# A spectral mix and a gated dense layer: early dense products spread over three phases, gates' loads and a gating product moved

## The chip, the cores and the metric

The kernel runs on one core of one Trainium2 chip. The metric is the device time of one execution in microseconds (us); lower is better. The engines are TensorE (PE), which multiplies; VectorE (DVE) and ScalarE (ACT), which split, add and evict; GpSimd (POOL) and SyncE (SP), which here only issue transfers, each through a queue of its own.

## The reference, cut to what matters

```python
x = A_x                                        # 1 x 2048 x 640
g = sigmoid((x * gate_w).sum(-1, keepdims=True))
a = einsum("bsd,ed->bse", x, dft_hid_re)
b = einsum("bsd,ed->bse", x, dft_hid_im)
y = einsum("ts,bse->bte", dft_seq_re, a) - einsum("ts,bse->bte", dft_seq_im, b)
h = einsum("bsd,df->bsf", x, w1) + b1          # 640 -> 1728
act = h * tanh(softplus(h))                    # mish
return g * y + (1 - g) * einsum("bsf,fd->bsd", act, w2)
```

All arrays are fp32.

## The kernel before, in words

**Stages.** The work is transposed: features lie on the 128 partitions, tokens in four groups t of 512 columns. Four stages follow each other on PE. The sequence stage multiplies x with the cosine and sine matrices (`sq`, four problems q: two halves of the tokens, real and imaginary part) and stores `usc`. The hidden stage (`hd`, two problems, one for each half of the tokens) multiplies that with the hidden matrices and stores y (`ysc`). The dense stage (`dense_first`, L816) makes the activations `asc`. The last stage (`ou`, two problems) multiplies them with w2, adds y and writes the output. Each problem is a two by two block product with seven instead of eight products (Winograd's form), so many operands are sums and differences that DVE makes. Each fp32 operand is split into a high and a low part in fp32r (`operand` L326, `split` L316: a copy on ACT, then a difference on DVE), and each product is three matmuls (`mm3` L341: high by high, high by low, low by high).

**A problem's phases.** `first` (L414) makes the product b11 and the fifth block row, over kh steps of k, into three banks, and copies them out (`to_sbuf` L313); with `aside` they go to HBM and come back later. `second` (L438) has three products (22, s2, s1), and prepares the lower weights for each k in `low` (L381): two loads into tiles of the pool x, four differences on DVE, five splits. `third` (L508) has the last three; its `done` (L555) and `give` (L563) evict the results, with a product by q where `q` is given: in the hidden stage that is g of the token group, broadcast over the partitions.

**The early part.** A share of the dense stage, that of the first six feature blocks (of 128) of w1 for the token groups 0 and 1, is computed between the first phases of the sequence stage. The order on PE is: sq[1].first, early_first (L730), sq[2].first, early_second (L762), sq[3].first, early_rests (L812), sq[0].first, and then second and third of each q. early_first has three units j of seven products over two of the five k; its results go to HBM (`early`). early_second has three units over the other three k, loads `early` back, adds, applies mish (`out_act` L662) and stores. `turns` (L725) lets the three units take one step each in turn. A unit of early_first uses three banks (b0, b1, b2), one of early_second four; PSUM has eight. `w1_twice` (L688) loads blocks of w1, forms sums t1 to t4 in tiles of the pool f, and splits them; `x_twice` (L712) does the same for x.

**Gates.** `gates` (L909) loads the gate weights once (`wide`) and x in token order in sixteen tiles of the pool x; one DVE instruction (L915) multiplies each by `wide` and sums it. g and 1 - g go to HBM as rows, from which they are broadcast.

**What sets the order.** All is written into a graph (`Graph` L48), and a planner (`run` L124) plays it forward with costs: a matmul 0.2267 us, ACT and DVE by their columns, a transfer 2.2 us plus its size at 370 GB/s. PE's order is that of the program. On ACT, DVE and the queues of SP and POOL the planner issues, whenever an engine is free, the ready operation with the earliest due time (`want`, worked out backwards from PE's times) for which tiles are free. The chip then executes each engine's instructions in that order. `by` sets a latest time by hand; gates' products have `GATES[0] + k * GATES[1]` = 120 + 10 k. Tiles are taken from pools in the plan: eight banks `psum`, 18 `f` (512 columns), 6 `x` (640 columns), 26 weight pairs `w`, 10 operand pairs `r`.

Of the kernel before, what the change touches and what calls it, by code (L numbers as in the profile page):

```python
# [12 lines left out]
OP = mybir.AluOpType  # L13
# [14 lines left out]
DELAY, RATE = 2.2, 370e3  # L28
GATES = 120.0, 10.0

# [8 lines left out]
class Op:  # L39


    def __init__(self, engine, emit, took, hold, at):
        self.engine, self.emit, self.took, self.hold, self.at = engine, emit, took, hold, at
        self.deps, self.after, self.vals = set(), [], []
        self.prompt, self.ends, self.want, self.psum, self.by = False, 0.0, None, False, 1e9


class Graph:  # L48
# [35 lines left out]
    def wants(self):  # L84
# [35 lines left out]
        for op in self.ops:  # L120
            if op.engine != "PE":
                op.want = max([op.want] + [(d.at if d.engine == "PE" else d.want) + d.took for d in op.deps])

    def run(self, pools):  # L124
# [22 lines left out]
        events, now, left, dma = [], 0.0, len(self.ops), 0.0  # L147

        def granted(op, blocked):
# [17 lines left out]
        while left:  # L167
            began = False
            for e, line in ready.items():
                if free[e] > now + 1e-9 or not line:  # L170
                    continue
                if e == "PE":
                    i = next((i for i, x in enumerate(line) if x[1] == pe[-1]), None)
                    if i is not None and not granted(self.ops[pe[-1]], set()):
                        i = None
                else:
                    blocked = set()
                    i = next((i for i, x in enumerate(line) if granted(self.ops[x[1]], blocked)), None)
                if i is None:
# [16 lines left out]
                else:  # L196
                    end = now + op.took + 0.03
                heapq.heappush(events, (end, op.n))
                left -= 1
                began = True  # L200
            if began:
                continue
            times = [t for e, t in free.items() if t > now + 1e-9 and ready[e]]
            if events:
                times.append(events[0][0])
            assert times, ("stuck", left, pe and self.ops[pe[-1]].at, [(p.name, len(p.free)) for p in pools])
            now = max(now, min(times))
            while events and events[0][0] <= now + 1e-9:
                op = self.ops[heapq.heappop(events)[1]]
# [18 lines left out]
def fnet_mish_gate(ctx: ExitStack, tc: tile.TileContext, xn, xt, c_re, c_im, wd_re, wd_im,  # L228
# [51 lines left out]

    def load(pool, src, of=None, rows=P, cols=N, queue="SP", by=1e9):
        v = Val(pool)
        op = dma(queue, lambda: ISSUE[queue].dma_start(v.t[:rows, :cols], src() if callable(src) else src),  # L283
                 whole(of) if of else [], whole(v), rows * cols * 4)
        op.by = by
        return v
# [119 lines left out]
    class Problem:  # L406
# [281 lines left out]
    def w1_twice(k0, fifth=False):  # L688

        C, w, at, n, tiles = slice(0, H * P), {}, {}, 0, []  # L690
        for i in range(2):
            for j in range(2):
                w[f"b{i + 1}{j + 1}"] = load(FS, w1h[k0 + i, j], cols=H * P)
        for o, x, y in (("t1", "b12", "b11"), ("t2", "b22", "t1"), ("t3", "b22", "b12"), ("t4", "b21", "t2")):
            w[o] = Val(FS)
            tt(w[o], w[x], w[y], OP.subtract, (C, C, C), n=H * P)
        if fifth:
            for j in range(2):
                w["d", j] = load(FS, w1h[KD - 1, j], cols=H * P)
        for o in ("b11", "b21", "t2", "t1", "t3", "t4", "b22") + (("d", 0), ("d", 1)) * fifth:  # L700
            i = 0
            while i < H:
                if n % KD == 0:
# [20 lines left out]

    def turns(units):  # L725
        units = list(units)
        while units:
            units = [u for u in units if next(u, u) is None]

    def early_first():  # L730

        at, x = w1_twice(0), x_twice(0)

        def unit(j):
            b0, b1, b2 = bank(), bank(), bank()
            mm3(b0, at["b11", j], x["a11"], True, True)
            p = to_sbuf(b0)
            yield
            mm3(b2, at["t1", j], x["s1"], True, True)
            yield  # L740
            mm3(b0, at["b21", j], x["a12"], False, True)
            store(early[0, j], to_sbuf(b0))
            yield
            copy(b1, p)
            mm3(b1, at["t2", j], x["s2"], False, True)
            u = to_sbuf(b1)
            yield
            mm3(b1, at["t3", j], x["s3"], False, True)
            v = to_sbuf(b1)
            tt(v, b2, v, OP.add)  # L750
            store(early[1, j + H], v)
            yield
            mm3(b1, at["t4", j], x["a22"], False, True)
            store(early[1, j], to_sbuf(b1))
            yield
            mm3(b2, at["b22", j], x["s4"], False, True)
            tt(u, b2, u, OP.add)
            store(early[0, j + H], u)
            yield
        turns(unit(j) for j in range(H))  # L760

    def early_second():  # L762
# [4 lines left out]
        def unit(j):  # L767
            b0, b1, b2, b3 = bank(), bank(), bank(), bank()

            def end(b, t, f):  # L770
                o = load_of(FS, early[t, f])
                tt(o, b, o, OP.add)
                out_act(f, t, o, o)
            mm3(b0, at["b11", j], x["a11"], True, True)
            p = to_sbuf(b0)
            yield
            mm3(b0, at["b21", j], x["a12"], False, False)
            mm3(b0, at[("d", 0), j], d[0], False, True)
            end(b0, 0, j)
            yield  # L780
            copy(b1, p)
            mm3(b1, at["t2", j], x["s2"], False, True)
            u = to_sbuf(b1)
            o = load_of(FS, early[0, j + H])
            tt(u, u, o, OP.add)
            yield
            mm3(b2, at["t1", j], x["s1"], True, True)
            yield
            mm3(b1, at["t3", j], x["s3"], False, True)
            v = to_sbuf(b1)  # L790
            tt(v, b2, v, OP.add)
            yield
            mm3(b1, at["t4", j], x["a22"], False, False)
            mm3(b1, at[("d", 0), j], d[1], False, True)
            end(b1, 1, j)
            yield
            mm3(b2, at["b22", j], x["s4"], False, False)
            mm3(b2, at[("d", 1), j], d[0], False, True)
            tt(u, b2, u, OP.add)
            out_act(j + H, 0, u, u)  # L800
            yield
            copy(b3, load_of(FS, early[1, j + H]))
            mm3(b3, at[("d", 1), j], d[1], False, True)
            tt(v, b3, v, OP.add)
            out_act(j + H, 1, v, v)
            yield
        turns(unit(j) for j in range(H))
        kept.update(x, d=d)

    kept = {}  # L810
# [98 lines left out]
    def gates():  # L909

        wide = load(X, gw.partition_broadcast(P), cols=D)
        tokens = xn.rearrange("k p d -> (k p) d").rearrange("(p k) d -> k p d", k=KS)
        for k in range(KS):
            x = load(X, tokens[k], cols=D)
            dve(lambda k=k, x=x: nc.vector.scalar_tensor_tensor(  # L915
# [23 lines left out]
    def put_out(d, t, f, queue=None):  # L939
# [5 lines left out]
    hd = [Problem(hid, tp, lambda t, k: load_of(FS, usc[k][t]), put_y, aside=aside("ph") if tp else None,  # L945
                  q=lambda t: keep(("g", t), lambda: broadcast(grow, t))) for tp in range(2)]
    ou = [Problem(fin, tp, lambda t, k: load_of(FS, asc[k][t]), put_out, rest=out_rest, aside=aside("po") if tp else None,
                  y=(lambda d, t: load_of(FS, ysc[d][t])) if tp else None,
                  q=None if tp else (lambda t: keep(("q", t), lambda: broadcast(qrow, t))), last=tp == 1) for tp in range(2)]
# [17 lines left out]
    for p in hd:  # L967
        p.second(hid.low)
        p.third()
    w1_rest(True)  # L970
    dense_first(0)
# [53 lines left out]
```

## Time and profile before

| | |
|---|---|
| median of three runs | 872.07 us (869.6 to 874.72) |
| the profiled execution | 874.41 us, of which the span from its first to its last instruction is 872.3 us |
| granted clock, mean | 0.996 |
| HBM traffic | 171.97 MB read, 42.22 MB written |

Times in rows of the profile are counted from the span's start. A row of the timeline has the start, the duration, the engine, the line, and the output and inputs by their tiles' names (f, x, w, r as the pools; ps is a bank; h and l are the high and the low part), and in brackets how long the engine had stood and what ended that. L337 is the matmul inside `mm`; L310 the ACT copy inside `copy`; L301 the DVE instruction inside `tt`; L331 and L332 the two halves of `operand`; L322 and L323 those of `split`; L283 a load, L293 a store.

### The profile page before, as it was taken

How to read it: one execution, taken by the hardware profiler on the slowest of the kernel's cores; microseconds unless marked ns; L12 is line 12 of the kernel's file. 1: busy time of each engine (PE TensorE's matmuls, PEld its weight loads, DVE VectorE, ACT ScalarE, POOL GpSimd, SP SyncE). 2: the span in 40 equal slices, each digit the busy share in tenths (PEclk: the TensorE clock that was granted, in tenths of full speed). 3: DMA queues.
4: the chain of work that ended last, by engine and by line, in shares of the span. 5: the costliest groups of instructions: out<-in, count | busy, mean ns of one | idle time of the engine just before them, and what ended most of it. 6: DMA issues, size and time to landing. Idle time of an engine off the chain costs nothing.

```text
span 872.3 us, 12120 instructions
## 1 busy us (share of the span) xinstructions
PE 859.0 (98%) x3754; PEld 705.2 (81%) x3754; DVE 697.2 (80%) x1241; ACT 485.9 (56%) x896; POOL 86.5 (10%) x157
## 2 busy tenths in 40 slices
PE   8998999999999999999999999999999999999998
PEld 6876888888888888888887888878888788888886
DVE  7888799987884887679998868998877996758493
ACT  7976486635353554456676634646666854533242
POOL 0312100002000200100020002022111200004000
PEclk9998999999999999999999999999999999999999
DMA  9999985867763966495677839587666886637943
GB/s 329 323 322 357 368 314 163 291 220 264 251 223 114 340 200 217 132 363 189 221 254 274 314 128 351 196 290 261 230 205 239 279 279 223 193 127 167 355 172 121
DMA packets 108704, 215.01 MB, mean 246 GB/s; under 512 B 13600, under 2 KB 17824, under 8 KB 108640
## 3 DMA queue, kind: packets, MB, share of 16 engines
q1 hardware_dynamic: 95744, 174.52, 59.0%
q0 software_dynamic: 12752, 39.59, 13.3%
q8 instruction: 29, 0.48, 0.2%
q14 instruction: 35, 0.29, 0.1%
q10 hardware_dynamic: 144, 0.13, 0.0%
HBM read 171.97 MB, written 42.22 MB: 246 GB/s over the span
## 4 chain that ended last, share of the span: by engine, by line
PE 87%; DVE 6%; DMA 4%; issue 1%; ACT 1%; SPq 0%; POOL 0%; ACTq 0%; DVEq 0%
PE ps L337 87%; DVE f L301 2%; DMA f<-in_c_im_dram 1%; DMA x<-in_w_dram 1%; DMA f<-in_xt_dram 1%; DMA ps<-f 1%; DVE x L301 1%; DMA f<-early 0%; ACT f L310 0%; DVE r1l L332 0%; DVE w13l L323 0%; SPq L283 0%; DVE w16l L323 0%; DVE r5l L332 0%; DVE w19l L323 0%
## 5 line engine op out<-in xcount | busy, mean ns | idle before, releaser
L301 DVE TENSOR_TENSOR f<-f,f 128x512 f32<-128x512 f32 (+2 forms) x327 | 218.1, 681 | 12.1 <-ACT f L606 4.2
L310 ACT ACTIVATE f<-ps 128x512 f32<-128x512 f32 x138 | 79.4, 595 | 24.6 <-PE ps L337 20.1
L301 DVE TENSOR_TENSOR f<-ps,f 128x512 f32<-128x512 f32 x108 | 70.8, 683 | 23.7 <-PE ps L337 17.0
L293 POOL DMA_DIRECT2D u<-f x40 | 21.6, 542 | 320.0 <-DVE f L301 309.3
L331 ACT ACTIVATE r1h<-f 128x512 fp32r<-128x512 f32 x40 | 25.2, 630 | 27.5 <-PE ps L337 16.5
L293 POOL DMA_DIRECT2D act<-f x52 | 28.2, 543 | 121.9 <-ACT f L606 53.4
L331 ACT ACTIVATE r3h<-f 128x512 fp32r<-128x512 f32 x38 | 23.9, 629 | 28.5 <-PE ps L337 18.4
L331 ACT ACTIVATE r2h<-f 128x512 fp32r<-128x512 f32 x39 | 24.5, 628 | 27.1 <-PE ps L337 18.9
L331 ACT ACTIVATE r8h<-f 128x512 fp32r<-128x512 f32 x38 | 23.9, 630 | 27.9 <-PE ps L337 16.2
L331 ACT ACTIVATE r6h<-f 128x512 fp32r<-128x512 f32 x37 | 23.3, 629 | 26.2 <-PE ps L337 19.1
L331 ACT ACTIVATE r0h<-f 128x512 fp32r<-128x512 f32 x39 | 24.5, 628 | 23.1 <-PE ps L337 11.5
L332 DVE TENSOR_TENSOR r0l<-f,r0h 128x512 fp32r<-128x512 f32 x40 | 27.5, 687 | 12.3 <-ACT r0h L331 12.1
L331 ACT ACTIVATE r5h<-f 128x512 fp32r<-128x512 f32 x38 | 23.9, 629 | 22.6 <-PE ps L337 13.0
L331 ACT ACTIVATE r7h<-f 128x512 fp32r<-128x512 f32 x39 | 24.5, 628 | 19.9 <-PE ps L337 9.7
L301 DVE TENSOR_TENSOR x<-x,x 128x256 f32<-128x256 f32 (+1 forms) x80 | 33.5, 434 | 2.4 <-DMA x<-in_w_dram 1.7
L331 ACT ACTIVATE r9h<-f 128x512 fp32r<-128x512 f32 x37 | 23.3, 629 | 21.2 <-PE ps L337 16.9
L332 DVE TENSOR_TENSOR r3l<-f,r3h 128x512 fp32r<-128x512 f32 x38 | 26.1, 687 | 11.0 <-ACT r3h L331 10.8
L332 DVE TENSOR_TENSOR r7l<-f,r7h 128x512 fp32r<-128x512 f32 x39 | 26.8, 687 | 9.9 <-ACT r7h L331 9.4
L310 ACT ACTIVATE ps<-f 128x512 f32<-128x512 f32 x57 | 33.5, 595 | 1.9 <-DVE f L301 1.7
L332 DVE TENSOR_TENSOR r2l<-f,r2h 128x512 fp32r<-128x512 f32 x39 | 26.8, 687 | 9.6 <-ACT r2h L331 9.2
L606 ACT ACTIVATE f<-f,b1s 128x512 f32<-128x512 f32 x36 | 25.8, 720 | 15.3 <-DVE f L301 14.7
L332 DVE TENSOR_TENSOR r1l<-f,r1h 128x512 fp32r<-128x512 f32 x40 | 27.5, 688 | 8.2 <-ACT r1h L331 7.8
(2225 smaller groups left out, 2689.3 us busy)
## 6 DMA issues: line engine op xcount, KB each, us to landing
f<-in_c_im_dram SPq DMA_DIRECT2D x128, 256.0 KB, 4.1
f<-in_c_re_dram SPq DMA_DIRECT2D x128, 256.0 KB, 4.4
f<-act SPq DMA_DIRECT2D x86, 256.0 KB, 4.3
f<-u SPq DMA_DIRECT2D x80, 256.0 KB, 5.3
act<-f POOLq DMA_DIRECT2D x52, 256.0 KB, 4.6
f<-in_xt_dram SPq DMA_DIRECT2D x42, 256.0 KB, 4.8
u<-f POOLq DMA_DIRECT2D x40, 256.0 KB, 5.2
x<-in_xn_dram SPq DMA_DIRECT2D x24, 320.0 KB, 5.3
```

The lines of the kernel that those rows point to most:

```text
L293: dma(queue, lambda: ISSUE[queue].dma_start(d.t, v.t[:rows]), whole(v), whole(d), rows * N * 4)
L301: dve(lambda: nc.vector.tensor_tensor(o.t[rows, x], a.t[rows, y], b.t[rows, z], op=op), whole(a, b), whole(o), n)
L310: act(lambda: nc.scalar.activation(o.t, a.t, AF.Copy, scale=scale), whole(a), whole(o))
L331: act(lambda: nc.scalar.activation(r.t[0][:, :N], src.t[:, :N], AF.Copy), whole(src), [(r, 0)])
L332: dve(lambda: nc.vector.tensor_tensor(r.t[1][:, :N], src.t[:, :N], f32(r.t[0][:, :N]), op=OP.subtract), whole(src) + [(r, 0)], [(r, 1)])
L337: G.add("PE", lambda: nc.tensor.matmul(bank.t, w.t[wn][:, k * P:k * P + P], x.t[xn_][:, :N], start, stop, skip_group_check=True), [(w, (k, ...
L606: act(lambda: nc.scalar.activation(o.t[rows], src.t[rows], AF.Mish, **more), whole(src, table) + whole(b1s) * bias, whole(o), more=0.1)
```

## The change

- **The early products.** early_first and early_second no longer run as blocks of their own. They return their units, and `first` becomes a generator (`steps`) that yields after each k. Two lines of units, [a0, a2, b1] and [a1, b0, b2] (a of early_first, b of early_second), take one step each after each k of the first phases of sq[2], sq[3] and sq[0]. early_rests comes after all of them.
- **Banks.** A unit has two banks, a and b. Where b1 was opened with a copy of p, now a itself is evicted and p copied back into it. The product t4 comes last, and the last block of early_second accumulates on a copy of v, with `early` added after it instead of before.
- **w1_twice** loads into tiles of the pool x, not f, writes t3 over b12 and t4 over b21, and interleaves sums with splits.
- **Gates.** Their loads have a time `since`, 110 + 10 k, before which the planner doesn't issue them; their products are due at 130 + 10 k.
- **y.** The hidden stage's second problem has no q: its y is stored ungated. `gate_y`, in the program ahead of the dense stage, loads these ten tiles again, multiplies them by g and stores them as `gysc`; due times 600 + 7 i. ou[1] reads `gysc`.
- **The planner** holds an operation of ACT or DVE that becomes ready well ahead of its due time: up to 1 us after an engine's work (CALM), up to 3 us after a transfer (CALM_DMA), less where it is due within 3 us more (NEAR). This changes the order of instructions; it adds none.

```diff
-GATES = 120.0, 10.0
+CALM, CALM_DMA, NEAR = 1.0, 3.0, 3.0
+GATES = 130.0, 10.0
+GATED = 600.0, 7.0
...
-                op.want = max([op.want] + [(d.at if d.engine == "PE" else d.want) + d.took for d in op.deps])
+                op.want = max([op.want, op.since] + [(d.at if d.engine == "PE" else d.want) + d.took for d in op.deps])
...
-                    i = next((i for i, x in enumerate(line) if granted(self.ops[x[1]], blocked)), None)
+                    i = next((i for i, x in enumerate(line)
+                              if self.ops[x[1]].since <= now and granted(self.ops[x[1]], blocked)), None)
...
-                        insort(ready[a.engine], (a.want, a.n))
+                        wait = min(CALM_DMA if op.engine in ("SP", "POOL") else CALM, a.want - now - NEAR)
+                        if a.engine in ("ACT", "DVE") and wait > 0:
+                            heapq.heappush(events, (now + wait, a.n, True))
+                        else:
+                            insort(ready[a.engine], (a.want, a.n))
...
         def first(self, top):
+            for _ in self.steps(top):
+                pass
+
+        def steps(self, top):
...
                     product(banks, blocks, x, k == 0, k == kh - 1)
+                yield
...
-                w[f"b{i + 1}{j + 1}"] = load(FS, w1h[k0 + i, j], cols=H * P)
-        for o, x, y in (("t1", "b12", "b11"), ("t2", "b22", "t1"), ("t3", "b22", "b12"), ("t4", "b21", "t2")):
-            w[o] = Val(FS)
-            tt(w[o], w[x], w[y], OP.subtract, (C, C, C), n=H * P)
+                w[f"b{i + 1}{j + 1}"] = load(X, w1h[k0 + i, j], cols=H * P)
...
+            if o in sums:
+                a, b = sums[o]
+                w[o] = {"t3": w["b12"], "t4": w["b21"]}.get(o) or Val(X)
+                tt(w[o], w[a], w[b], OP.subtract, (C, C, C), n=H * P)
...
     def early_first():
...
         def unit(j):
...
+            a, b = bank(), bank()
+            mm3(a, at["b11", j], x["a11"], True, True)
+            p = to_sbuf(a)
+            yield
+            mm3(b, at["t1", j], x["s1"], True, True)
+            yield
+            mm3(a, at["b21", j], x["a12"], False, True)
+            store(early[0, j], to_sbuf(a))
+            copy(a, p)
+            yield
+            mm3(a, at["t2", j], x["s2"], False, True)
+            u = to_sbuf(a)
+            yield
+            mm3(a, at["t3", j], x["s3"], False, True)
+            v = to_sbuf(a)
+            tt(v, b, v, OP.add)
             store(early[1, j + H], v)
             yield
...
+            mm3(b, at["b22", j], x["s4"], False, True)
+            tt(u, b, u, OP.add)
             store(early[0, j + H], u)
             yield
-        turns(unit(j) for j in range(H))
+            mm3(a, at["t4", j], x["a22"], False, True)
+            store(early[1, j], to_sbuf(a))
+            yield
+        return [unit(j) for j in range(H)]
...
     def early_second():
...
+            mm3(b, at["b22", j], x["s4"], False, False)
+            mm3(b, at[("d", 1), j], d[0], False, True)
+            tt(u, b, u, OP.add)
+            end(u, 0, j + H)
+            yield
+            mm3(a, at["t4", j], x["a22"], False, False)
+            mm3(a, at[("d", 0), j], d[1], False, True)
+            end(a, 1, j)
+            yield
+            copy(b, v)
+            mm3(b, at[("d", 1), j], d[1], False, True)
+            end(b, 1, j + H)
+            yield
...
-        wide = load(X, gw.partition_broadcast(P), cols=D)
+        wide = load(X, gw.partition_broadcast(P), cols=D, since=GATES[0] - 20)
...
-            x = load(X, tokens[k], cols=D)
+            x = load(X, tokens[k], cols=D, since=GATES[0] - 20 + k * GATES[1])
...
-                  q=lambda t: keep(("g", t), lambda: broadcast(grow, t))) for tp in range(2)]
+                  q=None if tp else lambda t: keep(("g", t), lambda: broadcast(grow, t))) for tp in range(2)]
+    gysc = {(d, t): dram(f"gy{d}_{t}") for t in (2, 3) for d in range(KD)}
+
+    def gate_y():
+
+        for i, ((d, t), o) in enumerate(gysc.items()):
+            v = load_of(FS, ysc[d][t])
+            tt(v, v, keep(("g", t), lambda: broadcast(grow, t)), OP.mult)
+            G.ops[-1].by = GATED[0] + GATED[1] * i
+            store(o, v)
...
-    early_first()
-    sq[2].first(seq_top)
-    early_second()
-    sq[3].first(seq_top)
+    ua, ub = early_first(), early_second()
+    lines = [ua[0], ua[2], ub[1]], [ua[1], ub[0], ub[2]]
+    lines = [(u for q in line for u in q) for line in lines]
+    for q in (2, 3, 0):
+        for _ in sq[q].steps(seq_top):
+            for line in lines:
+                next(line, None)
+    for line in lines:
+        for _ in line:
+            pass
     early_rests()
-    sq[0].first(seq_top)
...
+    gate_y()
     w1_rest(True)
```

More of the change, by code (lines that the diff above doesn't have):

```diff
@@ L44, in __init__ @@
         self.deps, self.after, self.vals = set(), [], []
[L45 removed]
+        self.prompt, self.ends, self.want, self.psum, self.by, self.since = False, 0.0, None, False, 1e9, 0.0
 class Graph:
@@ L147, in run @@
         events, now, left, dma = [], 0.0, len(self.ops), 0.0
+        waits = sorted({op.since for op in self.ops})
         def granted(op, blocked):
@@ L197, in run @@
                     end = now + op.took + 0.03
-                heapq.heappush(events, (end, op.n))
+                heapq.heappush(events, (end, op.n, False))
                 left -= 1
@@ L203, in run @@
             times = [t for e, t in free.items() if t > now + 1e-9 and ready[e]]
+            times += [t for t in waits if t > now][:1]
             if events:
@@ L208, in run @@
             while events and events[0][0] <= now + 1e-9:
-                op = self.ops[heapq.heappop(events)[1]]
+                _, n, held = heapq.heappop(events)
+                op = self.ops[n]
+                if held:
+                    insort(ready[op.engine], (op.want, op.n))
+                    continue
                 for v in op.vals:
@@ L279, in fnet_mish_gate, with load @@
     ISSUE = {"SP": nc.sync, "POOL": nc.gpsimd}
-    def load(pool, src, of=None, rows=P, cols=N, queue="SP", by=1e9):
+    def load(pool, src, of=None, rows=P, cols=N, queue="SP", by=1e9, since=0.0):
         v = Val(pool)
@@ L284, in load @@
                  whole(of) if of else [], whole(v), rows * cols * 4)
-        op.by = by
+        op.by, op.since = by, since
         return v
@@ L699, in w1_twice @@
                 w["d", j] = load(FS, w1h[KD - 1, j], cols=H * P)
-        for o in ("b11", "b21", "t2", "t1", "t3", "t4", "b22") + (("d", 0), ("d", 1)) * fifth:
+        sums = {"t1": ("b12", "b11"), "t2": ("b22", "t1"), "t3": ("b22", "b12"), "t4": ("b21", "t2")}
+        for o in ("b11", "b21", "t1", "t2", "t3", "t4", "b22") + (("d", 0), ("d", 1)) * fifth:
             i = 0
+            if o in sums:
+                a, b = sums[o]
+                w[o] = {"t3": w["b12"], "t4": w["b21"]}.get(o) or Val(X)
+                tt(w[o], w[a], w[b], OP.subtract, (C, C, C), n=H * P)
             while i < H:
@@ L723, in x_twice @@
         return x
[L725 to L728, printed above, removed]
     def early_first():
@@ L767, in unit, with end @@
         def unit(j):
-            b0, b1, b2, b3 = bank(), bank(), bank(), bank()
-            def end(b, t, f):
+            a, b = bank(), bank()
+            def end(c, t, f):
                 o = load_of(FS, early[t, f])
-                tt(o, b, o, OP.add)
+                tt(o, c, o, OP.add)
                 out_act(f, t, o, o)
-            mm3(b0, at["b11", j], x["a11"], True, True)
-            p = to_sbuf(b0)
+            mm3(a, at["b11", j], x["a11"], True, True)
+            p = to_sbuf(a)
@@ L776, in unit @@
             yield
-            mm3(b0, at["b21", j], x["a12"], False, False)
-            mm3(b0, at[("d", 0), j], d[0], False, True)
-            end(b0, 0, j)
+            mm3(b, at["t1", j], x["s1"], True, True)
             yield
[L781 to L785, printed above, removed]
+            mm3(a, at["b21", j], x["a12"], False, False)
+            mm3(a, at[("d", 0), j], d[0], False, True)
@@ L786, in unit @@
+            end(a, 0, j)
+            copy(a, p)
             yield
-            mm3(b2, at["t1", j], x["s1"], True, True)
+            mm3(a, at["t2", j], x["s2"], False, True)
+            u = to_sbuf(a)
             yield
-            mm3(b1, at["t3", j], x["s3"], False, True)
-            v = to_sbuf(b1)
-            tt(v, b2, v, OP.add)
+            mm3(a, at["t3", j], x["s3"], False, True)
+            v = to_sbuf(a)
+            tt(v, b, v, OP.add)
             yield
-            mm3(b1, at["t4", j], x["a22"], False, False)
@@ L801, in unit @@
+            mm3(a, at[("d", 0), j], d[1], False, True)
+            end(a, 1, j)
             yield
[L802 to L805, printed above, removed]
+            copy(b, v)
+            mm3(b, at[("d", 1), j], d[1], False, True)
+            end(b, 1, j + H)
             yield
-        turns(unit(j) for j in range(H))
         kept.update(x, d=d)
+        return [unit(j) for j in range(H)]
```

25 lines of the change are left out of this document (1 added, 24 removed).

## The prediction

> **What bounds the kernel now.** I read the page first, then who TensorE (PE) waited for, then the stages that hold those waits, then the order of time around the longest.
>
> ```profile
> span 872.3 us, 12120 instructions
> PE 859.0 (98%) x3754; PEld 705.2 (81%) x3754; DVE 697.2 (80%) x1241; ACT 485.9 (56%) x896; POOL 86.5 (10%) x157
> PEclk9998999999999999999999999999999999999999
> ```
>
> PE is busy nearly throughout, so only the time in which it stands or is slowed can be won. Count it. Eight of the 3754 matmuls are the warm-up of L893; 3746 belong to the products, and the diff neither adds nor removes one (early_first keeps 7 triples a unit, early_second 11). The chain of waits, the timeline's start and its end give:
>
> ```profile
> 694.43 173.97 PE ps L337 x766
> ```
> ```profile
> 4.75 0.70 PE L337 MATMUL ps<-r0h,w0h 128*128 128x512 f32 x2 [0.40 <-DVE r0h L329]
> 8.16 0.50 PE L337 MATMUL ps<-r1l,w1h 128*128 128x512 f32 x1 [0.22 <-DVE r1l L332]
> 868.00 0.39 PE L337 MATMUL ps<-w0h,w15l 128*128 128x512 f32 x1
> ```
>
> An unbroken stretch takes 173.97 / 766 = 0.227 us a matmul, so 3746 need 850.7. From the first (4.75) to the end of the last one's slot (868.23) passed 863.5. So 12.8 are lost, of which 1.8 before 8.16, at the kernel's head (the first seven take 3.4 and need 1.6). **About 11 us can be won, 1.3%; the floor of the profiled execution is 874.41 - 11.0 = 863.4.** The stages with a loss, as a table of 25 us windows (window, then busy time by engine, clock, DMA share, GB/s):
>
> ```profile
> 50.00:75.00 25.00, 21.18 (x80) 16.19 (x80) 20.19 (x44) 17.25 (x36) 3.23 (x6) 0.89 0.98 339
> 75.00:100.00 25.00, 25.00 (x109) 20.61 (x109) 20.52 (x39) 14.99 (x25) 5.02 (x10) 0.98 0.97 340
> 475.00:500.00 25.00, 24.42 (x108) 19.87 (x107) 20.54 (x36) 16.36 (x30) 1.62 (x3) 1.00 0.82 287
> 575.00:600.00 25.00, 23.00 (x100) 18.36 (x99) 25.00 (x52) 15.66 (x34) 6.55 (x13) 1.00 0.81 289
> 675.00:700.00 25.00, 24.50 (x107) 19.63 (x106) 24.09 (x48) 21.18 (x42) 5.40 (x10) 1.00 0.83 276
> ```
>
> Standing: 3.82 at 50-75, 0.58 at 475, 2.00 at 575, 0.50 at 675. Clock: (1-0.89) x 25 + (1-0.98) x 25 = 3.25, behind the first of them. Together 10.2; the rest of the 11 is slow restarts. So the early stage holds 7.1 of it and the border from the hidden stage to the dense one 2.0. What happened early, in order of time:
>
> ```profile
> 66.30 0.40 PE L337 MATMUL ps<-r2h,w13l 128*128 128x512 f32 x1
> 67.25 0.63 ACT L331 ACTIVATE r5h<-f 128x512 fp32r<-128x512 f32 x1 [1.78 <-DMA f<-in_c_im_dram]
> 67.47 0.33 SPq L283 DMA_DIRECT2D x<-in_xn_dram  x1
> 68.73 0.63 ACT L331 ACTIVATE r6h<-f 128x512 fp32r<-128x512 f32 x1 [0.86 <-DMA f<-in_c_im_dram]
> 69.27 1.55 ACT L310 ACTIVATE f<-ps 128x512 f32<-128x512 f32 x3
> 69.90 0.80 PE L337 MATMUL ps<-r2h,w13h 128*128 128x512 f32 x1 [3.21 <-ACT f L310]
> 71.78 0.63 PE L337 MATMUL ps<-w18l,w9h 128*128 128x512 f32 x1
> 72.20 0.63 PE L337 MATMUL ps<-w18h,w9l 128*128 128x512 f32 x1
> ```
>
> PE waits for evictions (f<-ps) that stand in ACT's order behind two operand copies, and those wait for cosine tiles still in flight. Afterwards matmuls come 0.42 apart instead of 0.227. The tiles are late because the transfer engines are full, and gates' loads go between them:
>
> ```profile
> DMA packets 14363, 30.96 MB, mean 344 GB/s; under 512 B 1883, under 2 KB 2651, under 8 KB 14354
> x<-in_xn_dram SPq DMA_DIRECT2D x17, 320.0 KB, 5.5
> f<-in_c_im_dram SPq DMA_DIRECT2D x8, 256.0 KB, 6.5
> x<-in_xn_dram SPq DMA_DIRECT2D x2, 256.0 KB, 5.8
> ```
> ```profile
> L915 DVE SCALAR_TENSOR_TENSOR x<-x,x x16: 809/817/826, 63.3 to 109.2; 128x640 f32<-128x640 f32 x16
> ```
>
> The first fence is the DMA view of 20-110 us (count, size, median us from issue to landing). All sixteen gates products run in 63-110, far ahead of need.
>
> **The change part by part.** *Gates held back.* Sixteen loads of 320 KB and sixteen products of 0.817 (plus a read of about 0.08) leave 63-110: 5.2 of the 31 MB, one sixth of a saturated stage, and 14.4 us of DVE. They return spread from 110 to about 280, into this (windows):
>
> ```profile
> 110.00:160.00 50.00, 50.00 (x223) 41.39 (x222) 48.50 (x106) 35.41 (x72) 1.12 (x2) 1.00 0.67 227
> 560.00:582.00 22.00, 20.17 (x88) 16.14 (x86) 22.00 (x49) 10.40 (x26) 5.36 (x10) 1.00 0.54 191
> 600.00:675.00 75.00, 75.00 (x333) 62.01 (x332) 55.48 (x99) 46.27 (x83) 13.56 (x25) 1.00 0.69 236
> ```
>
> The transfers have room there (0.67). DVE has not: five products by 160 are 4.5 us in a stage with 1.5 idle. The cover is the lead of the operands; the smallest stretch of it I found:
>
> ```profile
> 156.88 0.68 DVE L332 TENSOR_TENSOR r6l<-f,r6h 128x512 fp32r<-128x512 f32 x1
> ```
> ```profile
> 164.71 0.39 PE L337 MATMUL ps<-r6l,w11h 128*128 128x512 f32 x1
> ```
>
> r6l is ready at 157.56 and used at 164.71: 7.15 of lead against 4.5 of work. I cost it at nothing; without the cover it costs up to 4.5. On SP's queue the sixteen loads now stand among sq[0]'s and sq[1]'s cosine loads: where one waits for an x tile, those behind it wait too, and the same lead pays for it.
>
> *The early products.* PE's sum stays. Before, three units of early_first open nine bank values, three of early_second twelve, where eight banks exist; afterwards two lines open four beside the first phase's three. A line's next step comes after 9 matmuls of the phase and 3 or 6 of the other line, 12 x 0.227 = 2.7 us or more; before, a unit's next step came after the two others', 6 x 0.227 = 1.4. So an eviction has twice the time to hide in. Against that a new tight place: `copy(a, p)` now follows the eviction of the same bank, two ACT instructions of this length:
>
> ```profile
> L310 ACT ACTIVATE f<-ps x33: 577/598/612, 21.9 to 100.3; 128x512 f32<-128x512 f32 x33
> ```
>
> 2 x 0.6 in 2.7 leaves 1.5 us less the handovers, six times. The added loads, stores and ACT copies of both units are the same in number as before. w1_twice's sums move from the f tiles to the x tiles, which gates no longer hold then, so cosine loads find f tiles sooner. I take the 7.1 as gone and put 1.8 on the other side for new short waits, three of the size at 475 (0.58); the bounds are 0 and all of 7.1 again.
>
> *Second half's y.* At the hidden stage's end:
>
> ```profile
> 572.11 0.52 ACT L322 ACTIVATE w20h<-x 128x384 fp32r<-128x384 f32 x1 [1.59 <-DMA x<-in_w1a_dram]
> ...
> 580.20 0.42 ACT L322 ACTIVATE w15h<-x 128x256 fp32r<-128x256 f32 x1 [6.09 <-DVE x L301]
> ```
> ```profile
> L301 DVE TENSOR_TENSOR f<-f,f 128x512 f32<-128x512 f32 x12 | 7.8, 681 | 0.0
> L301 DVE TENSOR_TENSOR f<-ps,f 128x512 f32<-128x512 f32 x10 | 6.4, 679 | 0.0
> L301 DVE TENSOR_TENSOR x<-x,x 128x256 f32<-128x256 f32 x9 | 3.5, 416 | 0.0
> ```
> ```profile
> PE ps L337 <- ACT w17h L331: 1.5, 1, 1.5
> ```
>
> ACT stood 6.09 for a DVE sum of w1_block, and w17h, for which PE waited, is behind it. Ahead of that sum on DVE are the final sums of hd[1] (DVE's groups at 550-582). Ten of them are products by g (six from banks, four from tiles): 10 x 0.68 = 6.8 of DVE go. Six copies of 0.6 come to ACT, which was idle anyway: 3.6 in 6.09. What would be late next are the w1a tiles: ACT waited for one of them, but eight us before the stall. I take 2.0 as gone. In the dense stage come ten loads (on SP), ten products (6.8 on DVE, which has 75 - 55.48 = 19.5 idle in 600-675) and ten stores (on POOL's queue): 5.2 MB at a share of 0.69. Its readers are in ou[1], 100 us later. Nothing.
>
> *The planner's holds (CALM).* They add no instruction; they change the order on ACT and DVE, everywhere. No row prices this. Below nothing it can win the 1.1 left at 475 and 675; above, one more stall like the early one, 7.1. I take nothing, since the long stage between shows PE busy without a gap:
>
> ```profile
> 110.00:460.00 350.00, 350.00 (x1546) 289.82 (x1545) 288.73 (x504) 194.76 (x354) 22.68 (x42) 1.00 0.69 235
> ```
>
> **Sum.** 874.41 - 7.1 - 2.0 + 1.8 = 867.1 against the profiled execution. The median of the three runs is 2.3 lower. If those runs differ in their stalls, the new kernel still gives 867.1; if in an offset, 864.8. I take the middle, **866.0**.
>
> [...]
>
> **The rivals.** *(a) Waits are exchanged.* The evict-and-copy pair is held up by an ACT instruction that waits for a tile. Held by 1.78 + 0.86 as above, with 1.4 to spare, PE stands 1.2; at four of the six places, 5 us: 871. For it: the trace's holds are of that size, and transfers stay full until about 100. Against: the loads held back, and the planner now puts landing-dependent work later.
>
> *(b) Slower: the stage behind.* early_rests now stands right ahead of sq[0].second, and `wide` and one gates tile take two of the six x tiles from 110 to 280. low(k) needs three, so one k is prepared at a time. A k then takes at least a landing of 5.8 plus four DVE sums of some 0.42 and splits, about 8, against 21 x 0.227 = 4.8 that PE needs. Five k behind by 3.2 are 16; less the lead of 7.15, 9 us, and 3 of clock: 866 + 12 = 878. It decides once DVE is more than 7.15 late. For it: DVE's 48.5 of 50. Against: without gates in 63-110, more of low can be done before 110, where DVE gains 14 us.
>
> *(c) It doesn't do what it says.* `since` holds a load in the plan only; if SP reaches it early, the collision stays and 2.0 are won at most: 872.07 - 2.0 = 870.1.
>
> [...]
>
> **How the numbers follow.** Forecast 0.52 (862 to 867.7); (a) 0.20 (868 to 872); (b) 0.20 (873 to 885); (c) 0.05; (d) 0.03. Half a per cent, 4.4 us, is about what a measurement of this kernel can tell from no change. Faster by more: the forecast and a little of (a), 0.54. Within: the rest of (a), (c), (d) and a little of (b), 0.28. Slower: 0.18. The range runs from 861.5 (floor 863.4 less most of the runs' offset) to 876.5, which leaves out the worse half of (b).
>
> **What would show it.** Right: no PE wait over 1 us in 25-125 and a clock of 1.00 there; gates products from 110 on; no ACT wait of 6 us ahead of w1_block's copies near 580; busy windows 600-675 with more DVE and full PE. Wrong: PE waits for ACT's ps<-f or f<-ps in 25-110 (a), PE waits for an operand in 120-170 (b), gates products still before 110 (c), a clock under 1.00 without a wait (d), or a new wait after 700, where this change should touch nothing but the order.

## The result, and the profile after

The median of five runs is **864.8 us** (864.55 to 866.31), against 873.49 (869.6 to 874.72) for five runs of the kernel before: a ratio of 0.9914, 95% interval 0.9889 to 0.9939. Forecast was 866.0. The profiled execution took 866.31, with a span of 864.5. The page:

```profile
span 864.5 us, 12193 instructions
PE 856.1 (99%) x3754; PEld 704.8 (82%) x3754; DVE 694.5 (80%) x1241; ACT 486.9 (56%) x902; POOL 91.8 (11%) x167
PE 97%; DMA 2%; DVE 0%; ACT 0%; issue 0%; SPq 0%; ACTq 0%; DVEq 0%
```

The matmuls are as many; ACT has six instructions more, POOL ten. The chain of work that ended last is now PE for 97% instead of 87%. The windows that held the losses:

```profile
50.00:75.00 25.00, 25.00 (x112) 20.71 (x111) 20.45 (x42) 19.74 (x41) 4.12 (x8) 1.00 0.92 326
75.00:100.00 25.00, 22.63 (x92) 17.88 (x91) 16.14 (x33) 15.25 (x29) 3.23 (x6) 0.93 0.86 303
475.00:500.00 25.00, 25.00 (x112) 20.67 (x112) 23.22 (x45) 16.97 (x34) 0.00 (x0) 1.00 0.87 292
575.00:600.00 25.00, 25.00 (x112) 20.69 (x111) 20.87 (x49) 18.05 (x42) 5.53 (x11) 1.00 0.86 308
675.00:700.00 25.00, 25.00 (x112) 20.68 (x111) 24.23 (x50) 16.58 (x33) 3.78 (x7) 1.00 0.91 317
```

Four of the five stages are full. What is left stands at 75-100: 2.37 idle and 0.07 x 25 = 1.75 of clock. The view of PE's waits names it, and the timeline of ACT shows why:

```profile
PE ps L350 <- ACT ps L323: 2.4, 2, 1.9
```
```profile
88.64 0.72 ACT L335 ACTIVATE w15h<-x 128x640 fp32r<-128x640 f32 x1
90.84 0.63 ACT L344 ACTIVATE r0h<-f 128x512 fp32r<-128x512 f32 x1 [1.48 <-DMA f<-in_xt_dram]
91.68 0.74 ACT L335 ACTIVATE w19h<-x 128x640 fp32r<-128x640 f32 x1 [0.21 <-DMA x<-in_w1a_dram]
92.33 0.58 ACT L323 ACTIVATE ps<-f 128x512 f32<-128x512 f32 x1
```

This is rival (a): for the longer of the two waits, the copy of p back into its bank (ps<-f) stands in ACT's order behind an operand copy and a split that wait for landings. The shorter, 0.5 at 86, was for such a copy too, but that one had itself waited for DVE's eviction of the bank. The transfers of 20-110 us are lighter, and gates' products (L927 here) run where the plan puts them:

```profile
DMA packets 13020, 26.75 MB, mean 297 GB/s; under 512 B 1863, under 2 KB 2794, under 8 KB 13012
```
```profile
L927 DVE SCALAR_TENSOR_TENSOR x<-x,x x16: 806/817/826, 120.4 to 267.4; 128x640 f32<-128x640 f32 x16
```
```profile
110.00:160.00 50.00, 50.00 (x223) 41.38 (x222) 46.31 (x94) 32.31 (x64) 3.58 (x7) 1.00 0.78 260
560.00:582.00 22.00, 22.00 (x98) 18.22 (x98) 21.45 (x45) 14.92 (x33) 5.38 (x10) 1.00 0.71 242
600.00:675.00 75.00, 75.00 (x331) 61.65 (x330) 59.92 (x108) 48.21 (x89) 17.84 (x33) 1.00 0.85 293
```

So far this looks like the forecast with its reasons. The experiments say otherwise about the reasons.

One more number of both traces matters below. In the view of waits, the rows in which ACT waits for a transfer add up to 31.2 us in 29 waits before, and to 11.4 in 18 after. The longest of each:

```profile
ACT w19h L322 <- DMA x<-in_xn_dram: 2.8, 1, 2.8
ACT w25h L322 <- DMA x<-in_w1a_dram: 2.8, 1, 2.8
```
```profile
ACT r0h L344 <- DMA f<-in_xt_dram: 1.5, 1, 1.5
ACT r9h L344 <- DMA f<-act: 1.4, 1, 1.4
```

### The profile page after: what moved, and what is told of

Same layout as the page of the kernel before. It is cut to its first block, busy times and chain, and to the rows that moved or that the text cites. A ratio compares the mean times of both kernels' runs of the same rounds, so it can differ in the third digit from the quotient of the medians.

```text
span 864.5 us, 12193 instructions
## 1 busy us (share of the span) xinstructions
PE 856.1 (99%) x3754; PEld 704.8 (82%) x3754; DVE 694.5 (80%) x1241; ACT 486.9 (56%) x902; POOL 91.8 (11%) x167
## 4 chain that ended last, share of the span: by engine, by line
PE 97%; DMA 2%; DVE 0%; ACT 0%; issue 0%; SPq 0%; ACTq 0%; DVEq 0%
PE ps L350 97%; DMA x<-in_xn_dram 1%; DMA x<-in_w1a_dram 1%; DMA f<-in_c_im_dram 1%; SPq L296 0%; DVE f L314 0%; DVE x L314 0%; DVE r1l L345 0%; DVE r4l L345 0%; ACT r1h L344 0%; ACT ps L323 0%; ACT w19h L335 0%; ACT f L323 0%; DVE f L601 0%; ACT f L599 0%
## 5 line engine op out<-in xcount | busy, mean ns | idle before, releaser
L314 DVE TENSOR_TENSOR f<-f,f 128x512 f32<-128x512 f32 (+1 forms) x322 | 214.2, 683 | 5.1 <-DMA f<-act 2.0
L323 ACT ACTIVATE f<-ps 128x512 f32<-128x512 f32 x149 | 87.1, 595 | 63.4 <-PE ps L350 58.0
L314 DVE TENSOR_TENSOR f<-ps,f 128x512 f32<-128x512 f32 x101 | 66.9, 685 | 44.2 <-PE ps L350 34.2
L344 ACT ACTIVATE r9h<-f 128x512 fp32r<-128x512 f32 x40 | 25.3, 631 | 29.0 <-PE ps L350 20.5
L314 DVE TENSOR_TENSOR x<-x,x 128x256 f32<-128x256 f32 (+2 forms) x88 | 38.0, 445 | 2.2 <-DMA x<-in_xn_dram 1.5
L344 ACT ACTIVATE r4h<-f 128x512 fp32r<-128x512 f32 x38 | 23.9, 630 | 24.3 <-PE ps L350 18.7
L345 DVE TENSOR_TENSOR r9l<-f,r9h 128x512 fp32r<-128x512 f32 x40 | 27.5, 686 | 10.5 <-ACT r9h L344 10.3
L344 ACT ACTIVATE r8h<-f 128x512 fp32r<-128x512 f32 x36 | 22.7, 630 | 21.2 <-PE ps L350 10.9
L345 DVE TENSOR_TENSOR r6l<-f,r6h 128x512 fp32r<-128x512 f32 x38 | 26.1, 686 | 10.4 <-ACT r6h L344 10.2
L624 ACT ACTIVATE f<-f,b1s 128x512 f32<-128x512 f32 x36 | 25.9, 718 | 14.1 <-DVE f L314 13.8
```

Of the source, the lines that this page charges most:

```text
L314: dve(lambda: nc.vector.tensor_tensor(o.t[rows, x], a.t[rows, y], b.t[rows, z], op=op), whole(a, b), whole(o), n)
L323: act(lambda: nc.scalar.activation(o.t, a.t, AF.Copy, scale=scale), whole(a), whole(o))
L344: act(lambda: nc.scalar.activation(r.t[0][:, :N], src.t[:, :N], AF.Copy), whole(src), [(r, 0)])
L345: dve(lambda: nc.vector.tensor_tensor(r.t[1][:, :N], src.t[:, :N], f32(r.t[0][:, :N]), op=OP.subtract), whole(src) + [(r, 0)], [(r, 1)])
L624: act(lambda: nc.scalar.activation(o.t[rows], src.t[rows], AF.Mish, **more), whole(src, table) + whole(b1s) * bias, whole(o), more=0.1)
```

## The experiments

Three theories stood at the start. Theory 1, mine: gates' loads made the cosine tiles late. Theory 2: the early steps and banks were the trouble. Theory 3: the planner's holds (CALM) do the work. Each run was timed beside the kernel before on the same chip; that one's median was 875.92, 875.32 and 875.0 us in the three groups of four, so times are compared within a group and ratios across them. The forecasts in us were counted from the lower medians above (872.07 and 873.49), so where a run lands just above a range, the ratio decides.

**First group: one part alone, or one part undone.**

`b_gates_held`: before, with the hold on gates.

```diff
-        wide = load(X, gw.partition_broadcast(P), cols=D)
+        wide = load(X, gw.partition_broadcast(P), cols=D, since=GATES[0] - 20)
...
-            x = load(X, tokens[k], cols=D)
+            x = load(X, tokens[k], cols=D, since=GATES[0] - 20 + k * GATES[1])
```

> The kernel before, with nothing but gates' loads held back (and their due times at 130 + 10 k). Theory 1 (gates' loads made the cosine tiles late, and ACT's order passed that on to PE): the loss at 64-76 us goes, no PE wait over 1 us in 25-125, clock 1.00 there; the wait near 580 stays; 866 to 868 us. Theory 2 (the banks and the short steps made it): PE still waits for ACT's evictions between 55 and 75, 871 to 874. Theory 3 (the planner's holds did it): as theory 2.

876.09 us, ratio 1.0001 (0.9973 to 1.0029): nothing. And the hold did what it says; gates' products ran from 122.7 to 271.2. In the window PE still stands 3.87 and loses 1.75 of clock, 5.6 of the 7.1 before, behind the same kind of instructions of ACT:

```profile
50.00:75.00 25.00, 21.13 (x83) 16.04 (x82) 22.78 (x50) 19.54 (x43) 3.23 (x6) 0.93 0.93 326
```
```profile
66.49 0.57 ACT L313 ACTIVATE f<-ps 128x512 f32<-128x512 f32 x1
68.35 0.63 ACT L334 ACTIVATE r5h<-f 128x512 fp32r<-128x512 f32 x1 [1.29 <-DMA f<-in_c_im_dram]
68.89 0.58 ACT L313 ACTIVATE f<-ps 128x512 f32<-128x512 f32 x1
```

Theory 1 falls as the main cause of the early loss. But the run does not show what earlier tiles would do, for those that ACT waits for here did not come earlier: in 20-110 the transfers still moved 29.08 MB (30.96 before), because other loads took part of the room (`in_c_re` 28 loads against 25, `in_xn` of 256 KB four against two), and the cosine loads of `in_c_im` landed in 6.8 us at the median (6.5 before; those of `in_c_re` in 4.7, 5.5 before). ACT's order still puts a copy that waits for a tile ahead of an eviction that PE waits for. At 475-500 this profile loses 4.3 (2.55 standing, 1.75 of clock), where the kernel before lost 0.6.

`a_gates_free`: after, with gates' loads free and due at 120 + 10 k.

```diff
-GATES = 130.0, 10.0
+GATES = 120.0, 10.0
...
-        wide = load(X, gw.partition_broadcast(P), cols=D, since=GATES[0] - 20)
+        wide = load(X, gw.partition_broadcast(P), cols=D)
...
-            x = load(X, tokens[k], cols=D, since=GATES[0] - 20 + k * GATES[1])
+            x = load(X, tokens[k], cols=D)
```

> The kernel after, with gates' loads free again (due times 120 + 10 k). Theory 1: gates' loads fall into 25-110 again, ACT waits there for cosine tiles, PE stands 3 us or more and loses clock: 868 to 873 us. Theory 2: the two lines have room for late evictions, 864 to 866. Theory 3: 864 to 866.

868.97 us, ratio 0.9912 (0.9883 to 0.9941). Theory 1 had the time, but no theory had the reason: the free loads did not fall into 25-110. The products ran from 114.9 to 141.9, probably because w1_twice now takes the x tiles before (its loads into them begin at 10.9; this was not tried apart). There they meet `low` of sq[0].second, and PE waits for a lower weight:

```profile
145.10 0.50 PE L350 MATMUL ps<-r5h,w4h 128*128 128x512 f32 x1 [1.04 <-ACT w4h L335]
145.43 0.40 PE L350 MATMUL ps<-r5l,w4h 128*128 128x512 f32 x1
146.47 0.50 PE L350 MATMUL ps<-r5h,w4l 128*128 128x512 f32 x1 [0.64 <-DVE w4l L336]
```

ACT also loads its tables for gates' sigmoid there (at 142.07 and 145.06, 1.28 us each; in the kernel after the two, L931 and L937, take 1.283 each), but the copy of w4h itself then stood 0.42 for a sum on DVE.

`a_steps_alone`: after, with gates free as above, the holds at zero and y gated in the hidden stage, so that steps, banks and w1_twice are left (ou[1] reads `ysc`).

```diff
-CALM, CALM_DMA, NEAR = 1.0, 3.0, 3.0
+CALM, CALM_DMA, NEAR = 0.0, 0.0, 3.0
...
-                  q=None if tp else lambda t: keep(("g", t), lambda: broadcast(grow, t))) for tp in range(2)]
+                  q=lambda t: keep(("g", t), lambda: broadcast(grow, t))) for tp in range(2)]
...
-    gate_y()
```

> The kernel after with only the early products' steps, banks and w1_twice: gates free, no holds of the planner, y gated in the hidden stage. Theory 1: waits of 3 us or more in 25-110 and the wait near 580: 870 to 874 us. Theory 2: clean to 125, only the wait near 580: 866 to 868. Theory 3: 870 to 874.

876.55 us, ratio 0.9993 (0.9966 to 1.002). Theory 2 falls too: in time, the steps alone are worth nothing. The trace says where their gain went. Early (25-175) PE loses 3.1 instead of 7.1, without loss of clock; but at 450-500 it stands 3.12 and loses 3.5 of clock, where the kernel before lost 0.6. There an eviction stands behind a split that waits for a sum on DVE, not for a landing:

```profile
475.67 0.42 ACT L335 ACTIVATE w20h<-x 128x256 fp32r<-128x256 f32 x1 [4.21 <-DVE x L314]
475.99 1.07 ACT L323 ACTIVATE f<-ps 128x512 f32<-128x512 f32 x2
476.62 0.80 PE L350 MATMUL ps<-r5h,w17h 128*128 128x512 f32 x1 [3.12 <-ACT f L323]
```

`a_no_calm`: after, with the holds at zero.

```diff
-CALM, CALM_DMA, NEAR = 1.0, 3.0, 3.0
+CALM, CALM_DMA, NEAR = 0.0, 0.0, 3.0
```

> The kernel after with the planner's holds set to zero. Theory 3: PE waits come back, in the early stage and at the borders: 868 to 873 us. Theories 1 and 2: within 1 us of the kernel after, 864 to 866.

874.07 us, ratio 0.997 (0.9951 to 0.9989). Most of the gain is gone with this one line. Beyond the head PE waits again six times, 8.7 us in all, early and at the borders:

```profile
PE ps L350 <- ACT ps L323: 5.2, 3, 2.8
PE ps L350 <- DVE f L314: 2.1, 2, 1.4
PE ps L350 <- ACT f L323: 1.4, 1, 1.4
```

ACT's waits for transfers add up to 32.2, as before the change. Theory 3 stands: without the holds the other parts together are worth 0.3%.

**Second group: adding up from before.**

`b_calm`: before, with the holds.

```diff
-                        insort(ready[a.engine], (a.want, a.n))
+                        wait = min(CALM_DMA if op.engine in ("SP", "POOL") else CALM, a.want - now - NEAR)
+                        if a.engine in ("ACT", "DVE") and wait > 0:
+                            heapq.heappush(events, (now + wait, a.n, True))
+                        else:
+                            insort(ready[a.engine], (a.want, a.n))
```

> The kernel before with nothing but the planner's holds. Theory 3 (the holds take the blocking instructions out of ACT's and DVE's order everywhere): 5 to 8 us under before, waits at 475, 675 and 693 gone, the early one mostly; the one near 580 stays or shrinks. Theory 4 (the holds only help together with the steps and the room in the tiles): within 2 us of before, early waits still 3 us or more.

869.89 us, ratio 0.9931 (0.9909 to 0.9953): 5.4 us, as theory 3 said. The waits at 475, 675 and 693 are gone, and those at the hidden stage's end stay. The early ones are not mostly gone, as theory 3 had it: they are shorter one by one (1.7 at most, 3.2 before) and cost no clock, but at 50-75 they still add up to 3.72 (3.82 before). PE's waits in 550-620:

```profile
PE ps L346 <- DVE w1l L341: 1.6, 1, 1.6
PE ps L346 <- ACT ps L319: 0.9, 1, 0.9
```

`b_calm_y`: the same, with y gated in the dense stage.

```diff
-                  q=lambda t: keep(("g", t), lambda: broadcast(grow, t))) for tp in range(2)]
+                  q=None if tp else lambda t: keep(("g", t), lambda: broadcast(grow, t))) for tp in range(2)]
...
+    gate_y()
     w1_rest(True)
```

> The kernel before with the holds and with the second half's y gated in the dense stage; early products, banks and gates' loads as before. Theory 3: within 1.5 us of the kernel after, no wait near 580. Theory 4: at least 4 us above the kernel after, with the loss between 25 and 110.

867.29 us, ratio 0.9898 (0.9874 to 0.9923): 2.6 less, and PE has no wait in 550-620. What is left of its losses is early, as ACT's evictions:

```profile
PE ps L347 <- ACT f L320: 3.8, 3, 1.8
PE ps L347 <- ACT ps L320: 0.8, 1, 0.8
```

`after_again`: the kernel after, beside them.

> The kernel after once more, as the reference for the runs beside it: 7 to 10 us under the kernel before.

865.83 us, ratio 0.9882 (0.9861 to 0.9903). So **of 9.5 us the holds give 5.4, y 2.6, and steps, banks, w1_twice and gates together 1.5**, each on top of those before it. The last is inside the spread: runs of `b_calm_y` reach from 866.27 to 868.51, those of the kernel after from 864.59 to 866.94.

`a_t1_between`: after, with b's first product between a's eviction and a's next use, in both kinds of unit.

```diff
-            mm3(b, at["t1", j], x["s1"], True, True)
-            yield
             mm3(a, at["b21", j], x["a12"], False, True)
             store(early[0, j], to_sbuf(a))
             copy(a, p)
             yield
+            mm3(b, at["t1", j], x["s1"], True, True)
+            yield
             mm3(a, at["t2", j], x["s2"], False, True)
```

> The kernel after with one exchange in every unit: the product t1 on bank b comes between b21 and t2 on bank a, so the eviction of a and the copy back into it have two intervals between steps instead of one (some 6 us for 2.7). If the evict-and-copy pair makes the waits at 85 and 91 us: they go, 1 to 4 us under the kernel after. If the copies stand behind blocked instructions for longer than that, or the next tight place takes over: within 1 us of it.

**864.49 us** (863.97 to 865.32), ratio 0.9868 (0.985 to 0.9887), the fastest of all: 1.3 under the kernel after beside it, though their ranges overlap. Against `b_calm_y` it is 2.8 less, and there the ranges do not meet, so with this exchange the early parts and gates together are worth something on top of the holds and y. In its profile the waits for ACT's ps<-f are gone; PE stands once more, 1.0, for an eviction:

```profile
PE ps L350 <- ACT f L323: 1.0, 1, 1.0
```
```profile
75.00:100.00 25.00, 24.03 (x107) 19.56 (x106) 18.64 (x37) 17.55 (x35) 4.05 (x8) 1.00 0.89 308
```

**Third group: what in the holds does it, and gates again.**

`b_calm_dma` and `b_calm_own`: `b_calm` with only one of the two holds.

```diff
-CALM, CALM_DMA, NEAR = 1.0, 3.0, 3.0
+CALM, CALM_DMA, NEAR = 0.0, 3.0, 3.0        # b_calm_dma
+CALM, CALM_DMA, NEAR = 1.0, 0.0, 3.0        # b_calm_own
```

> The kernel before with the holds after transfers alone (CALM 0, CALM_DMA 3). If the holds work because tiles land later than the planner assumes: most of what both holds gave (5.4 us), so 4 to 5.5 us under before. If they work through the order among ACT's and DVE's own instructions: within 2 us of before.

> The kernel before with the holds after an engine's own work alone (CALM 1, CALM_DMA 0). If late landings are the cause: within 2 us of before. If the order among the engines' own instructions is: 4 to 5.5 us under it.

868.86 us, ratio 0.9928 (0.9905 to 0.995), and 873.82 us, ratio 0.9975 (0.9949 to 1.0001). The hold after transfers gives 6.1 alone, as much as both, which is what the expectation said for late landings as the cause. The hold after the engines' own work gives 1.2 by the medians, not to be told from nothing (its interval reaches 1.0001).

`b_delay`: before, without holds, the planner's latency of a transfer nearer to what the traces show.

```diff
-DELAY, RATE = 2.2, 370e3
+DELAY, RATE = 4.5, 370e3
```

> The kernel before, without holds, with the planner's latency of a transfer raised from 2.2 to 4.5 us, about what the transfers' median to landing shows. If the planner's early landings are the cause: 3 to 6 us under before, ACT's waits for transfers at least a third smaller. If only a hold on what isn't due soon does it: within 2 us of before.

878.39 us, ratio 1.0046 (1.0029 to 1.0063): slower, which neither expectation had. ACT's waits for transfers fell from 31.2 to 14.1, more than the hold after transfers achieves in `b_calm_dma` (21.7), and the time went the other way. PE waits for evictions in 25-125 all the same, loses clock at 50-75 and at 575-600, and stands at 825 for the first time:

```profile
PE ps L337 <- ACT f L310: 5.5, 3, 2.0
```
```profile
50.00:75.00 25.00, 21.00 (x83) 16.30 (x82) 21.35 (x49) 17.37 (x37) 3.24 (x6) 0.93 1.04 392
575.00:600.00 25.00, 21.54 (x86) 16.75 (x85) 23.90 (x50) 13.90 (x29) 5.67 (x11) 0.93 0.82 293
825.00:850.00 25.00, 24.46 (x104) 18.96 (x104) 21.52 (x36) 10.82 (x19) 0.00 (x0) 1.00 0.73 244
```

No ACT instruction in front of those three early evictions waited for a landing; at 61.84 and 75.14 one waited for a sum on DVE instead (0.62 and 0.95). So fewer waits for landings are not enough; an eviction can stand behind other instructions too. That a late landing costs nothing as such is not shown: changing the latency also moves loads and due times everywhere, and which of its shifts made the new waits was not tried apart.

`a_gates_free_2`: `a_gates_free` once more, beside the other before.

> The kernel after with gates' loads free again, a second time, since the first ran in another call than the kernel after (ratios 0.9912 against 0.9914 and 0.9882). If the hold on gates is worth something here: 1 to 3 us above the kernel after, ratio 0.990 to 0.993, with waits near 143 us or in 25-110. If not: ratio 0.987 to 0.990.

869.37 us, ratio 0.993 (0.9903 to 0.9956). The two ratios, 0.9912 and 0.993, lie above those of the kernel after, 0.9914 and 0.9882, by 0.2% on average; the intervals overlap. PE's waits near 143 came back in this profile too: 2.2 for ACT's w4h and 0.6 for DVE's w4l, after 1.0 and 0.6 in the first. By these waits the hold on gates is worth 1.6 to 2.8 us here, once the other parts are in; the times do not contradict that, and do not settle it.

## Why the prediction was right, and where its reasons were not

**The account of PE's losses held.** From 4.84, the first product, to 860.52, the end of the last one's slot, the kernel after spends 855.7 for 850.7 of work. That is 5.0 lost, 1.5 of it in the head and 3.5 behind (the window 75-100 alone gives 4.1, so the account is good to about half a us); forecast were 11 - 7.1 - 2.0 + 1.8 = 3.7. Against the profiled execution 867.1 was expected and 866.31 came. The gain was 8.1 between the profiled executions and 8.7 between the medians, for 7.3 forecast.

**The step that failed is "The planner's holds: I take nothing", and with it the cause of the early 7.1.** The holds alone gave 5.4 us of 9.5; gates' hold alone left the ratio at 1.0001, the steps alone at 0.9993, neither to be told from nothing. Holding gates back did not even free 5.2 MB, nor make the cosine tiles that ACT waits for earlier (6.8 us to landing, 6.5 before; `b_gates_held`). The profile's row was read rightly, an eviction behind an operand copy that waits for a tile, but I asked only what would make the tile earlier. The copy could have stood behind: r5h, made at 67.25 while the eviction waited, is first read by PE 18 us later:

```profile
85.83 0.39 PE L337 MATMUL ps<-r5h,w1h 128*128 128x512 f32 x1
```

That the order is the cause rests on `b_calm_dma`, which adds and removes no instruction and gains 6.1, and on the stalls in `b_delay` and `a_steps_alone`, where evictions stand behind waits for DVE. It does not make lateness harmless: in `b_calm` PE still stands 1.67 at 73.67, behind an operand copy (r7h) that waits 2.23 for its tile. The profiles, one of each run, show what each part does where (standing + clock lost, in us, counted by 25 us windows as in the prediction):

| | 25-175 | 450-500 | 550-600 | 650-725 |
|---|---|---|---|---|
| before | 3.8 + 3.3 | 0.6 | 2.0 | 0.5 |
| `b_calm` (holds) | 3.7 | 0 | 2.5 | 0 |
| `b_calm_y` (holds, y) | 4.6 | 0 | 0 | 0 |
| `a_steps_alone` | 3.1 | 3.1 + 3.5 | 1.8 | 1.3 |
| `a_no_calm` (all but holds) | 5.2 | 1.4 | 0 | 2.1 |
| after | 2.4 + 1.8 | 0 | 0 | 0 |
| `a_t1_between` | 1.0 | 0 | 0 | 0 |

So neither the holds nor the steps clear the early stage alone. In these profiles the holds (`b_calm`) take the loss of clock there and the 1.1 at 475 and 675 that I gave them as the least; with the steps but no holds, what is won early is lost again at 476. I argued for nothing from the quiet stage 110-460. It says little about the others: ACT evicts 51 banks to tiles in its 350 us, but 29 in the 85 us of 25-110.

That the total came out is therefore in part luck: the term that I set to nothing carried more than half of the gain, and the parts that I credited with 7.1 gave nothing alone. They happened to be changed together.

**y was right**: 2.0 forecast, 2.6 measured on top of the holds, with the wait near 580 gone and its DVE work hidden at 600-675 (55.48 to 59.92 busy, PE full).

**Rival (a) came to pass at two of its six places.** In the profile after, the evict-and-copy pair costs 2.4 of standing and some 1.8 of clock, where the allowance for new waits was 1.8; the 1.1 at 475 and 675, which I had left standing, went too and made up for part of it. One exchange of steps removes these waits.

**Rival (b) had the place and the wrong sign.** sq[0].second after early_rests is tight, but it is early gates products that hurt it (115-142, in `a_gates_free`); the hold spreads them to 267. DVE is 46.31 busy there instead of 48.50.

**Rival (c) did not happen**: no gates product ran before 120.4. **Rival (d)**, a clock under 1.00 without a wait, given 0.03, did not either: in the profile after the clock is 1.00 in every 25 us window but 75-100 (0.93, behind the wait of 1.85) and the last (0.97), in which PE's matmuls still come 0.227 apart until they end at 860.52.

## What to carry to other kernels

Where an engine executes in order, as ACT did here (evictions behind a copy that waited 1.78 us for its tile), read what stands ahead of the late instruction, and ask whether that was due at all; taking other loads out of the way may not even make its input earlier, as holding gates back did not here (6.8 us to landing against 6.5). A planner that places work as soon as its model calls it ready fills queues with instructions that can block; holding those that aren't due was worth more here than all the rearrangement of steps and banks (5.4 us against 1.5, gates' loads among the latter). And a part that is worth nothing alone (the steps, 0.9993) may still be part of the fastest version, so undo parts as well as adding them, and read where the loss went when the time stays the same.

## What the runs showed of the hardware

In these profiles the clock of PE did not follow the length of a wait alone. In the kernel after, a wait of 1.85 us was followed by matmuls at 0.43 apart; in `a_no_calm`, one of 2.83 left the clock at 1.00 (window 50-75):

```profile
92.96 0.50 PE L350 MATMUL ps<-r6h,w25h 128*128 128x512 f32 x1 [1.85 <-ACT ps L323]
93.30 0.40 PE L350 MATMUL ps<-r6l,w25h 128*128 128x512 f32 x1
93.54 0.48 PE L350 MATMUL ps<-r6h,w25l 128*128 128x512 f32 x1
93.82 0.63 PE L350 MATMUL ps<-r7h,w3h 128*128 128x512 f32 x1
94.25 0.63 PE L350 MATMUL ps<-r7l,w3h 128*128 128x512 f32 x1
```
```profile
64.52 0.50 PE L350 MATMUL ps<-r7h,w21h 128*128 128x512 f32 x1 [2.83 <-ACT ps L323]
64.85 0.40 PE L350 MATMUL ps<-r7l,w21h 128*128 128x512 f32 x1
65.09 0.39 PE L350 MATMUL ps<-r7h,w21l 128*128 128x512 f32 x1
65.32 0.40 PE L350 MATMUL ps<-r9h,w3h 128*128 128x512 f32 x1
```

In the kernel before, the wait of 3.21 was followed by matmuls at 0.42 apart, and the 2.00 at 575-600, two waits of 1.5 and 0.5, left the clock at 1.00. With the 1.85 and the 2.83 beside them, these few waits give no length from which the clock falls; what else decided it was not shown. Of the five runs of the kernel after, three had a mean clock of 1.000 and 864.55 to 864.8 us, and two 0.998 and 865.54 and 866.31.
